# A linear-attention and shrink kernel: another way to compute the shrink, and seven products for eight in three more units

## The chip, the cores and the metric

The kernel runs on one core of one Trainium2 chip. Its time is the device time of one execution in microseconds (us). Four runs of the kernel before gave a median of 559.51 us, from 558.82 to 560.05. A core has TensorE (matrix products, PE in the profile, its weight loads PEld), VectorE (DVE), ScalarE (ACT), GpSimd (POOL), and SyncE (SP), whose queue issues most DMAs here.

## The reference

A recurrent linear attention with gates (GLA), followed by two dense layers with the shrink x - tanh(x) between them. All in 4-byte floats in the kernel; the dense weights come as 8-byte floats.

```
# q, k, v, alpha: (4, 8, 768, 48)
for t in range(S):
    state = alpha[:, :, t, :, None] * state + einsum('bhd,bhe->bhde', k[:, :, t], v[:, :, t])
    y[:, :, t] = einsum('bhd,bhde->bhe', q[:, :, t], state)
x = y.transpose(0, 2, 1, 3).reshape(3072, 384)
h = x @ w_in                # (384, 2048)
g = h - tanh(h)
return g @ w_out            # (2048, 384)
```

## The kernel before

The 3072 rows are worked in 12 units of 256 rows (`NU`, `TU`); a unit is two chunks of 128 rows. For each unit there is a GLA part and a dense part (`moe`). The GLA part of a unit runs some one and a half units ahead of its dense part.

The GLA part loads q, k and alpha so that VectorE can transpose them in blocks (`widen` on ScalarE, then `flip`), makes running products of alpha by two scans (`scan_U`, `scan_W`), multiplies k and q by them, and then needs TensorE for the scores, the new state and the result, which is `xT` of the unit (`scores`, `masked`, `mid`, `state`, `x`, `rest`).

The dense part of a unit has 8 steps (`FS`), each for 256 of the 2048 columns of `w_in`:

- the first product `h` = w_in.T x, 256 columns of w_in by 256 rows, over three tiles of 128 features (`KT`). In units 0 to 5 it is six products of 256 columns (`first`, L1256). From unit 6 on (`SEVEN = 6`) the first two feature tiles are taken as a 2 by 2 product of 128-blocks with seven products of 128 columns instead of eight, the third tile as two products of 256 columns (`seven_a`, `product`, `seven_d`, `seven_e`, L1267 and L1288). The seven products need sums of weight blocks (`weigh`) and of row blocks (`mix`). One PSUM bank holds `h`; four partial sums are copied out of it by ScalarE in three copies between the products (`keep`, L1278 and L1280), and VectorE adds them to the bank's content at the end (`join`, L1293);
- the shrink: u is a multiple of h squared (`square`, ScalarE, L1299), z a square of a linear function of u (`quadratic`, ScalarE, L1303), w = h u (`cube`, VectorE, L1308), g = (z + constant) w (`shrunk`, VectorE, L1312). So g is a polynomial of h that stands for h - tanh(h) while h is small. After every second step ScalarE checks that all u were small enough (`large`, L1318); if one was not, the whole result is computed again by a general path;
- the second product g times w_out. In units 0 and 1 (`PLAIN = 2`) four products of 384 columns (L1336); from unit 2 on seven products of 192 columns (L1358), of sums of blocks of g (`sums`, L1325 and L1326) and of weights (`combine`).

At the end of a unit, `store` adds up the output banks (L1418 on ScalarE, four times L1421 on VectorE) and writes out four pieces by DMA.

The weights come in 16 pieces through four buffers; ScalarE and VectorE turn the 8-byte floats into 4-byte floats (`round_weight`, L88, L89 on ScalarE, L91, L92 on VectorE). Later all pieces are loaded once more and ScalarE looks whether a value was out of range (`too_wide`, L106, L107).

Every piece of work is a task with a name, an engine, and what it comes after. The order in which the tasks are issued is written out by hand: `Planner.STEPS` holds it as differences of task numbers. So each engine's queue, in which instructions run strictly in order, is fixed by that list. PSUM has two banks with the tag "h", in turn for `h` of the steps and for results of the GLA part. The tiles `u`, `w` and `z` have two buffers, `g` three.

Of the kernel before, what the change touches and what calls it, by code (L numbers as in the profile page):

```python
# [1 line left out]

# [14 lines left out]
P = 128  # L17
# [12 lines left out]
U_FAST = 1.0 / 32  # L30
QA, QB, QK = 0.2301250865552381, -0.2896718893320786, 0.24942350940007277
# [39 lines left out]
def round_weight(nc, pool, raw, dst):  # L71

    V, A = nc.vector, nc.scalar
    n = dst.shape[-1]
    if raw.dtype == FP32:  # L80
        A.mul(dst, raw.rearrange("p (j n) -> p j n", n=n), W_SCALE)
        yield
        return
    lo, hi = words(raw)
    bits = pool.tile([P, WN], I32, name="bits")
    more = pool.tile([P, WN], I32, name="more")
    halves = more.bitcast(mybir.dt.int16).rearrange("p (n two) -> p n two", two=2)
    A.activation(halves[:, :, 0], lo, AF.Copy, scale=2.0 ** -29)  # L88
    A.activation(halves[:, :, 1].bitcast(mybir.dt.float16), hi.bitcast(FP32), AF.Sign)  # L89
    yield  # L90
    V.tensor_scalar(out=bits, in0=hi, scalar1=3, scalar2=None, op0=ALU.logical_shift_left)  # L91
    V.tensor_add(dst.bitcast(I32), bits.rearrange("p (j n) -> p j n", n=n),  # L92
                 more.rearrange("p (j n) -> p j n", n=n))
# [6 lines left out]
def too_wide(nc, junk, raw, most, least):  # L100


    A = nc.scalar
    junk = junk[:, 0:WN]
    src = raw if raw.dtype == FP32 else words(raw)[1].bitcast(FP32)
    A.activation(junk, src, AF.Abs, accum_out=most)  # L106
    A.activation(junk, junk, AF.Relu, scale=-1.0, bias=LEAST if raw.dtype != FP32 else -1.0, accum_out=least)  # L107
# [214 lines left out]
class Planner:  # L322
# [6 lines left out]
        "90 2 -1 3 -1 3 4 -3 9 26 -37 8 30 -26 7 -10 -6 12 24 -29 12 1 -17 -101 99 20 -10 -1 4 8 3 5 -26 9 2 23 -7 -5 -121 127 12 -3 -18 24 -7 -137 114 7 13 14 "  # L329
        "-24 6 -129 114 -110 120 -122 142 2 -1 367 -387 10 -132 145 365 -506 131 381 -5 -375 2 375 -511 137 373 -366 -139 143 364 3 -514 144 -137 509 -371 370 "  # L330
        "-513 515 3 -372 -2 -141 144 -146 7 140 5 363 -512 520 -5 -508 -5 514 -10 -501 -2 7 507 -370 -141 515 -376 382 -2 -512 137 -4 -138 143 371 -374 365 5 "
        "-507 -2 7 136 376 -516 511 10 -514 511 -516 515 -5 7 -12 -502 -2 7 512 6 -522 135 383 -511 -5 134 381 -9 11 -509 513 -520 2 519 -387 391 -520 -2 519 "
        "-11 -505 520 -518 127 392 -4 -5 -382 392 -519 508 -507 520 -1 4 -394 -2 4 -1 399 -401 396 -523 524 -366 -27 404 -6 -368 -29 -131 532 -20 -354 -26 403 "
        "-374 368 -10 -360 365 -391 397 -367 377 -15 -391 402 1 -392 -6 -2 389 -361 366 -396 406 2 2 -404 25 381 -407 2 -4 55 340 9 6 -386 -19 -7 402 -347 353 "
        "6 3 -4 -350 -53 405 -404 -3 8 408 -396 390 2 -361 360 -363 347 -372 391 3 2 -1 -412 23 384 -389 3 26 349 -377 -21 5 -2 401 -378 -25 23 392 -563 174 "
        "391 -390 344 -350 -168 175 390 -564 566 2 -3 -9 -365 -15 -1 -24 416 -415 25 16 -40 409 -380 16 -18 43 -26 7 365 -391 21 26 -44 2 12 376 -344 -43 386 "
        "-346 -45 23 376 -6 -571 230 343 -1 -367 373 -577 584 -3 -2 -1 -572 199 368 7 11 -364 347 -376 387 2 -12 17 2 -8 10 -3 -5 11 -396 5 374 7 -582 588 11 "
        "-405 399 -3 -589 594 -1 -18 24 -408 -198 610 -3 1 -607 204 397 -600 587 -366 -41 43 388 -4 -601 246 -24 390 -611 605 -431 25 28 367 8 5 -432 74 339 18 "
        "-388 394 4 -21 13 6 -389 21 367 -10 6 -608 221 -25 418 5 -400 -218 249 366 10 -380 374 -397 -24 23 400 -13 18 -423 21 2 394 8 -12 14 -3 -5 -371 378 -6 "
        "10 -632 630 -14 -615 199 433 2 -1 2 3 -440 -1 3 2 434 -433 443 -417 410 2 -1 3 -642 224 428 -6 -645 224 422 1 -27 32 4 -28 12 2 12 -1 -428 423 1 10 "  # L340
        "-658 241 -14 -25 23 3 15 -42 -200 633 25 -456 458 -428 427 -412 394 12 -382 -18 411 -420 -243 654 -383 376 13 -410 414 -663 273 387 11 -7 3 -419 -4 "
        "421 -390 379 12 -395 401 -426 422 6 -1 -12 -414 -246 668 6 -425 2 -250 674 -448 49 393 8 -452 5 -2 -2 459 -7 2 -1 3 -1 -679 690 -9 3 -683 685 -436 435 "
        "6 -17 13 -436 441 1 -5 7 3 -4 2 9 -6 2 -1 -698 680 24 -703 705 -1 6 -3 -8 1 -451 462 2 -1 5 -451 2 -17 -25 -225 251 21 25 388 32 4 -720 255 437 -467 "
        "52 427 -456 -22 492 -1 -417 406 -453 459 -444 431 -448 3 43 -22 432 -706 718 -6 8 3 -722 254 14 32 -45 457 -442 26 427 -451 -22 21 454 -5 4 -448 -2 "
        "-273 728 -3 -5 -419 -300 735 -10 3 2 -451 450 3 -1 -456 458 3 -10 12 -1 -461 463 1 -463 -276 741 -740 253 -1 24 17 6 449 -494 487 -463 -308 773 -1 3 "
        "-450 460 -6 2 -7 -418 -325 749 -450 432 -408 432 2 -756 758 19 -16 -457 451 -5 -420 414 24 -17 11 -436 -49 486 -481 17 465 14 -483 442 32 10 -6 -804 "
        "354 -322 779 -480 445 36 -24 25 -477 447 13 5 13 -12 -12 -431 438 30 -12 -12 25 -12 -482 495 -38 26 13 -25 13 -485 487 26 -15 -12 -21 49 -515 500 -11 "
        "1 26 -15 16 -15 16 -44 29 16 -15 2 -1 3 12 -45 46 -542 543 -15 16 -32 18 16 7 -555 1 514 32 9 -551 569 -571 554 -41 59 -26 -32 41 -552 570 -26 9 -531 "
        "549 -17 -528 546 -17 -532 533 17 -46 30 17 -16 28 -11 -15 -1 28 -59 34 -1 -32 47 12 -58 33 26 -12 -553 555 -1 2 10 -9 -36 -504 -40 24 521 45 -589 590 "
        "-547 548 -590 544 1 46 -30 -537 16 552 10 18 -24 -34 -492 493 40 -10 -29 57 -27 -569 579 -559 577 -43 -510 536 18 -17 -26 27 17 -16 32 -15 -574 558 "  # L350
        "-14 31 -551 535 17 -30 14 -583 21 24 555 -15 -1 -31 48 12 -614 -1 4 552 32 17 -33 32 3 26 -44 -16 43 -611 569 -571 631 -59 31 11 18 -615 570 28 -600 "
        "618 -17 -28 29 17 -16 17 -617 24 577 17 1 -17 -597 566 16 -15 31 17 -614 599 -602 628 -10 28 -17 -44 16 19 -1 11 17 -61 45 -28 -599 644 -16 -11 -34 1 "
        "61 -45 29 -11 28 -16 -45 46 16 -624 625 -16 17 -30 -618 632 -639 656 -15 -1 17 -15 17 8 -643 2 581 -623 624 60 -7 24 -16 -26 -34 -553 630 -76 60 -12 "
        "-649 678 -16 -686 641 62 -28 12 -686 703 -658 596 63 -17 1 -12 29 -654 638 17 -632 -32 600 76 -75 47 -32 61 -12 -15 -621 588 97 -48 28 -16 -8 -52 -611 "
        "612 60 -44 33 -19 31 15 -28 -31 45 -30 45 -14 15 -28 -635 603 15 -14 60 -27 12 16 -695 696 -718 702 17 -714 -7 705 30 -13 -15 -34 63 -30 -32 49 -701 "
        "731 -26 10 -62 1 78 -62 46 -14 1 -675 689 -713 -1 730 -62 47 16 -15 16 -15 16 -50 -678 729 -731 732 -17 -687 638 1 31 -17 -704 739 17 -15 -1 17 -34 "
        "-18 56 -758 703 -705 -3 709 51 -50 51 -760 768 -25 43 -25 8 -44 62 -43 -18 37 7 18 -61 44 -766 723 61 -758 741 18 -61 -702 746 18 -17 -746 764 -17 18 "
        "-17 -31 49 -17 -748 750 -1 17 -15 19 -3 9 -758 2 748 -51 60 -59 -741 742 59 -26 42 -15 -44 34 26 -15 -44 -733 768 10 15 -14 -778 793 -819 759 -712 773 "
        "-819 804 16 1 -62 46 -753 770 -779 791 -28 -32 34 -33 48 12 -59 -726 786 -12 28 -15 -60 51 -21 31 -13 -32 60 19 -78 45 -13 28 -14 -31 46 -60 32 29 -60 "
        "14 47 -16 -12 29 -16 17 -814 798 -32 34 28 -61 48 14 -61 31 31 -14 30 -869 792 62 16 -30 -32 33 -816 818 12 -31 47 -62 33 30 -62 15 31 -45 62 -29 13 "  # L360
        "17 -848 832 17 1 -17 -33 -795 846 -50 -819 852 -831 -23 872 -16 -1 21 -3 9 -25 17 -52 -819 820 -825 860 -19 44 -8 25 -896 880 -7 -37 61 -16 -44 -842 2 "
# [72 lines left out]
def fast(tc, q, k, v, alpha, moe_w_in, moe_w_out, out, w_in, w_out, ident, ok, pad_rows):  # L434
# [7 lines left out]
    NU = B * UPB  # L442
    KT, d_ff = w_in.shape[1], w_in.shape[2]
    FT, d_model = w_out.shape[1], w_out.shape[2]
    FS = FT // 2
    NH = d_model // 2
    PLAIN = 2
    SEVEN = 6
    BOTH_QUEUES = 0
    V, A, T, GP = nc.vector, nc.scalar, nc.tensor, nc.gpsimd  # L450

    out_r = out.rearrange("(t p) n -> t p n", p=P)

    with ExitStack() as ctx:
# [782 lines left out]
        def moe(u, rank, gait):  # L1237
# [6 lines left out]
            def step(s):  # L1244
# [37 lines left out]
                def seven_d():  # L1282
                    for n, to in ((2, 0), (3, 1), (4, 2)):
                        product(n, to)
# [269 lines left out]
```

## Time and profile before

The profiled execution took 561.18 us, of which 559.4 us are the span from the first instruction to the last.

| what | value |
|---|---|
| median of four runs | 559.51 us |
| profiled execution, its span | 561.18 us, 559.4 us |
| granted TensorE clock | 0.999 |
| VectorE: `cube` (L1308) | 96 x 0.68 us |
| VectorE: `shrunk` (L1312) | 96 x 0.683 us |
| ScalarE: `square` (L1299), `quadratic` (L1303) | 96 x 0.609 us, 96 x 0.630 us |
| ScalarE: `large` (L1318) | 48 x 1.054 us |
| VectorE: `flip` (L699) | 120 x 0.625 us |

In the page, an engine's busy time is the time in which at least one of its instructions runs. Two instructions of one engine overlap a little, so the sum of an engine's durations is more than its busy time. A matmul of 4-byte floats is two instructions, each with a weight load. In the rows of groups, the first number after the bar is the group's busy time, then the mean of one in ns, and after the second bar how long the engine was idle just before, with what ended it.

### The profile page before, as it was taken

The page shows a single profiled execution, that of the slowest core. Times are in us where ns is not written, and L with a number is a line of the kernel's source. Part 1 is how long each engine was busy: PE and PEld are TensorE (multiplying, and loading weights), DVE is VectorE, ACT ScalarE, POOL GpSimd, SP SyncE. Part 2 cuts the span into 40 slices and gives each one's busy share as a digit, 9 for nine tenths or more (in the row PEclk, how much of TensorE's full clock was granted, in tenths as well). Part 3 has the DMA queues.
Part 4 walks back from the last instruction along what each step waited for, and adds up shares of the span by engine and source line. Part 5 has one row for each costly group of instructions (what it writes and reads, how often), then busy time and mean ns, then how long its engine had stood idle before and what let it go on. Part 6 is the DMA issues. An engine that isn't in the chain of part 4 may idle for free. (4 is left out here: it accounts for less than half of the span.)

```text
span 559.4 us, 14664 instructions
## 1 busy us (share of the span) xinstructions
PE 547.2 (98%) x6045; PEld 496.0 (89%) x6045; DVE 462.5 (83%) x853; ACT 357.7 (64%) x722; POOL 4.9 (1%) x23
## 2 busy tenths in 40 slices
PE   8999999999999999999999999999999999999995
PEld 6786677778998999999999999999999999999995
DVE  7978889999998498588896799999899856765764
ACT  3688996648676766776794556767555544545550
POOL 3000000000000000000000000000000000000000
PEclk9999999999999999999999999999999999999999
DMA  9899882135582483453550041221100100000001
GB/s 237 189 248 247 271 176 58 30 93 142 107 166 65 106 196 116 114 127 121 163 144 0 30 94 30 61 62 30 47 19 1 31 8 3 29 8 1 29 2 33
DMA packets 60233, 50.86 MB, mean 91 GB/s; under 512 B 35552, under 2 KB 49920, under 8 KB 60160
## 3 DMA queue, kind: packets, MB, share of 16 engines
q1 hardware_dynamic: 57536, 49.07, 35.0%
q8 instruction: 49, 0.80, 0.6%
q10 hardware_dynamic: 2624, 0.79, 0.6%
q14 instruction: 24, 0.20, 0.1%
HBM read 44.04 MB, written 4.72 MB: 87 GB/s over the span
## 5 line engine op out<-in xcount | busy, mean ns | idle before, releaser
L1256 PE MATMUL h<-xT,w_in 128*128 128x256 f32 (+1 forms) x588 | 131.4, 378 | 2.8 <-DVE w_in L92 2.0
L1256 PEld LDWEIGHTS h<-xT,w_in 128*128 128x128 f32 x588 | 108.3, 190 | 18.9 <-DVE w_in L92 3.6
L1358 PE MATMUL o<-b,e 128*128 128x192 f32 x480 | 93.2, 326 | 0.0
L1358 PEld LDWEIGHTS o<-b,e 128*128 128x128 f32 x480 | 78.9, 190 | 0.4
L1358 PE MATMUL o<-w_out,e 128*128 128x192 f32 x320 | 78.6, 328 | 0.1
L1312 DVE SCALAR_TENSOR_TENSOR g<-z,w 128x512 f32<-128x512 f32 x96 | 64.8, 683 | 6.0 <-ACT z L1303 2.3
L1358 PE MATMUL o<-b,g 128*128 128x192 f32 x320 | 68.7, 326 | 0.0
L1303 ACT ACTIVATE z<-u 128x512 f32<-128x512 f32 x96 | 60.3, 630 | 4.2 <-DVE g L1312 2.6
L1293 DVE TENSOR_TENSOR w<-h,u 128x512 f32<-128x512 f32 x48 | 33.0, 688 | 34.1 <-PE h L1288 34.1
L1299 ACT ACTIVATE u<-w 128x512 f32<-128x512 f32 x48 | 30.0, 627 | 41.9 <-DVE w L1293 41.7
L1358 PEld LDWEIGHTS o<-w_out,e 128*128 128x128 f32 x320 | 55.0, 190 | 1.5 <-issue 0.2
L1267 PE MATMUL h<-xT,w_in 128*128 128x128 f32 x288 | 54.7, 277 | 0.2
L1280 ACT COPY u<-h 128x128 f32<-128x128 f32 x96 | 24.6, 266 | 46.8 <-PE h L1267 46.6
L1358 PEld LDWEIGHTS o<-b,g 128*128 128x128 f32 x320 | 53.8, 190 | 0.1
L1267 PE MATMUL h<-xT,w_out 128*128 128x128 f32 x288 | 53.3, 275 | 0.0
L1318 ACT ACTIVATE big<-u 128x1024 f32<-128x1024 f32 x48 | 50.6, 1054 | 0.6
L1267 PEld LDWEIGHTS h<-xT,w_in 128*128 128x128 f32 x288 | 48.1, 190 | 2.4 <-ACT xT L1038 0.4
L1288 PE MATMUL h<-xT,w_in 128*128 128x256 f32 x192 | 48.9, 380 | 0.0
L1299 ACT ACTIVATE u<-h 128x512 f32<-128x512 f32 x48 | 28.3, 590 | 29.8 <-PE h L1256 29.6
L1325 DVE TENSOR_TENSOR e<-g 128x384 f32<-128x384 f32 x80 | 44.0, 550 | 2.6 <-PE o L1358 0.8
L1308 DVE TENSOR_TENSOR w<-h,u 128x512 f32<-128x512 f32 x48 | 32.5, 681 | 14.8 <-ACT u L1299 14.8
L1267 PEld LDWEIGHTS h<-xT,w_out 128*128 128x128 f32 x288 | 44.1, 192 | 0.1
(171 smaller groups left out, 967.7 us busy)
## 6 DMA issues: line engine op xcount, KB each, us to landing
raw<-in_moe_w_out_dram SPq DMA_DIRECT2D x16, 768.0 KB, 5.9
raw<-in_moe_w_in_dram SPq DMA_DIRECT2D x48, 96.0 KB, 5.2
raw<-in_moe_w_in_dram SPq DMA_DIRECT2D x16, 288.0 KB, 5.2
vt<-in_v_dram SPq DMA_DIRECT2D x23, 192.0 KB, 3.6
ar<-in_alpha_dram SPq DMA_DIRECT2D x20, 192.0 KB, 3.4
kr<-in_k_dram SPq DMA_DIRECT2D x20, 192.0 KB, 3.3
qr<-in_q_dram SPq DMA_DIRECT2D x20, 192.0 KB, 3.2
raw<-in_moe_w_in_dram SPq DMA_DIRECT2D x16, 192.0 KB, 6.0
```

What stands on the lines that cost most here:

```text
L1256: T.matmul(h[:, a, to], lhsT=w_in[:, j, f * P:(f + 1) * P], rhs=xT[u][:, j, to], start=(j == 0), stop=(j == KT - 1))
L1267: T.matmul(m["h", s][:, to], lhsT=left[n][:, s], rhs=right[u][n], start=start, stop=True, skip_group_check=True)
L1280: A.copy(m["kept", s][:, n], m["h", s][:, 3])
L1288: T.matmul(m["h", s][:, 2 * a:2 * a + 2].rearrange("p i t -> p (i t)"), lhsT=wi[:, KT - 1, s, a], rhs=xT[u][:, KT - 1, :], start=False, st ...
L1293: V.tensor_add(m["w", s], m["h", s].rearrange("p i t -> p (i t)"), m["u", s])
L1299: A.activation(m["u", s], m["h", s], AF.Square, scale=W_SCALE ** -1.5)
L1303: A.activation(m["z", s], m["u", s], AF.Square, bias=QB, scale=QA * W_SCALE)
L1308: V.tensor_mul(m["w", s], m["h", s], m["u", s])
L1312: V.scalar_tensor_tensor(out=g.rearrange("p a c t -> p (a c t)"), in0=m["z", s], scalar=QK, in1=m["w", s], op0=ALU.add, op1=ALU.mult)
L1318: A.activation(big, m["us", s // 2].rearrange("p s t -> p (s t)"), AF.Relu, bias=-U_FAST, scale=W_SCALE, accum_out=over[:, n:n + 1])
L1325: V.tensor_sub(e[:, 0:3, :], x[:, 3:4].to_broadcast([P, 3, P]), x[:, 0:3])
L1358: T.matmul(o[n][:, i], lhsT=g_, rhs=w_, start=(s_ == 0 and (n, i) in ((0, 0), (1, 0), (2, 1), (3, 0))), stop=(s_ == FS - 1), skip_group_ch ...
```

## The change

Five things are changed:

1. The shrink. ScalarE computes z = tanh(TA h), then z = arctan(TB z), then u, a multiple of z squared (`bend`, `turn`, `square`); VectorE multiplies once, g = h u (`shrunk`). `cube` and `quadratic` are gone. The check `large` compares with the new function's value at the same h.
2. `SEVEN` is 3: units 3, 4 and 5 too take seven products.
3. The seven products use two banks. Four go into the four quarters of a first bank (`seven_a`); ScalarE copies one quarter out, and VectorE makes the four partial sums with three additions (`partial`). The other three and the third feature tile go into a second bank (`seven_b`); `join` adds the two.
4. Tasks are cut finer: the two ScalarE reads and the two VectorE operations of a weight piece, the two copies of `widen`, the four transposes of `flip`, the halves of the scans of units 1 to 11, the two looks at a reloaded piece, the five operations of a unit's `store`. In the last unit the last operation is done in two halves, each with its own DMAs right behind it. The looks write over the piece that they read instead of using another tile.
5. `STEPS` is another list, for the new tasks.

```diff
-U_FAST = 1.0 / 32
-QA, QB, QK = 0.2301250865552381, -0.2896718893320786, 0.24942350940007277
+TA, TB, TK = 0.524562418460846, 1.0865100622177124, 1.0129976272583008
+F_FAST = (TK * atan(TB * tanh(TA * 2.0 ** -2.5))) ** 2
...
-    SEVEN = 6
+    SEVEN = 3
...
                 def seven_a():
-                    m["h", s] = ps_h.tile([P, 4, P], FP32, name="h")
-                    product(1, 3, True)
-                    product(5, 1)
-
-                def keep(n):
-                    if n == 0:
-                        take_u()
-                        m["kept", s] = m["u", s].rearrange("p (i t) -> p i t", t=P)
-                        A.copy(m["kept", s][:, 0::3], m["h", s][:, 3::-2])
-                    else:
-                        A.copy(m["kept", s][:, n], m["h", s][:, 3])
-
-                def seven_d():
-                    for n, to in ((2, 0), (3, 1), (4, 2)):
-                        product(n, to)
-
-                def seven_e():
+                    h = m["part", s] = ps_h.tile([P, 4, P], FP32, name="h")
+                    for i, n in enumerate((1, 6, 7, 5)):
+                        T.matmul(h[:, i], lhsT=left[n][:, s], rhs=right[u][n], start=i == 0, stop=True, skip_group_check=True)
+
+                def keep():
+                    take_u()
+                    m["kept", s] = m["u", s].rearrange("p (i t) -> p i t", t=P)
+                    A.copy(m["kept", s][:, 0], m["part", s][:, 0])
+
+                def partial():
+                    kept, part = m["kept", s], m["part", s]
+                    V.tensor_add(kept[:, 1], kept[:, 0], part[:, 1])
+                    V.tensor_add(kept[:, 2], kept[:, 1], part[:, 2])
+                    V.tensor_add(kept[:, 1::2], kept[:, 1:3], part[:, 3:4].to_broadcast([P, 2, P]))
+
+                def seven_b():
+                    h = m["h", s] = ps_h.tile([P, 4, P], FP32, name="h")
+                    for i, n in enumerate((2, 3, 4)):
+                        T.matmul(h[:, i], lhsT=left[n][:, s], rhs=right[u][n], start=i == 0, stop=True, skip_group_check=True)
                     for a in range(2):
-                        T.matmul(m["h", s][:, 2 * a:2 * a + 2].rearrange("p i t -> p (i t)"), lhsT=wi[:, KT - 1, s, a], rhs=xT[u][:, KT - 1, :],
+                        T.matmul(h[:, 2 * a:2 * a + 2].rearrange("p i t -> p (i t)"), lhsT=wi[:, KT - 1, s, a], rhs=xT[u][:, KT - 1, :],
                                  start=False, stop=True, skip_group_check=True)
...
+                def bend():
+                    m["z", s] = two.tile([P, 2 * TU], FP32, name="z")
+                    A.activation(m["z", s], m["h", s], AF.Tanh, scale=TA / W_SCALE)
+
+                def turn():
+                    A.activation(m["z", s], m["z", s], AF.Arctan, scale=TB)
+
                 def square():
                     if not seven:
                         take_u()
-                    A.activation(m["u", s], m["h", s], AF.Square, scale=W_SCALE ** -1.5)
-
-                def quadratic():
-                    m["z", s] = two.tile([P, 2 * TU], FP32, name="z")
-                    A.activation(m["z", s], m["u", s], AF.Square, bias=QB, scale=QA * W_SCALE)
-
-                def cube():
-                    if not seven:
-                        m["w", s] = two.tile([P, 2 * TU], FP32, name="w")
-                    V.tensor_mul(m["w", s], m["h", s], m["u", s])
+                    A.activation(m["u", s], m["z", s], AF.Square, scale=TK * W_SCALE ** -0.5)
 
                 def shrunk():
                     g = m["g", s] = three.tile([P, 2, CU, P], FP32, name="g")
-                    V.scalar_tensor_tensor(out=g.rearrange("p a c t -> p (a c t)"), in0=m["z", s], scalar=QK,
-                                           in1=m["w", s], op0=ALU.add, op1=ALU.mult)
+                    V.tensor_mul(g.rearrange("p a c t -> p (a c t)"), m["h", s], m["u", s])
...
-            add(f"read {what}{s}", "ACT", 2.1, rank, [f"fetch {what}{s}", both and f"upper {what}{s}", older and f"{older[0]}{older[1]}"], a)
-            add(f"{what}{s}", "DVE", 1.6, rank, [f"read {what}{s}"], b)
+            add(f"read_a {what}{s}", "ACT", 1.05, rank, there, lambda do=do: do(0))
+            add(f"read {what}{s}", "ACT", 1.05, rank, [f"read_a {what}{s}"], lambda do=do: do(1))
+            add(f"bits {what}{s}", "DVE", 0.6, rank, there, lambda do=do: do(2))
+            add(f"{what}{s}", "DVE", 1.0, rank, [f"read {what}{s}", f"bits {what}{s}"], lambda do=do: do(3))
...
+                elif u < NU - 1:
+                    put(same, o[0][:, 0:1, :].to_broadcast([P, 2, NH]), ALU.add, same, 0)
+                else:
                     for c in range(CU):
...
+                        put(same[:, c], o[0][:, 0, :], ALU.add, same[:, c], 0, [c])
```

## The prediction

> **What bounds the kernel now.** I read the page's first part, then busy time by stretches of 20 us, then the timeline of single engines where it is densest. The first line is the whole span; the others give a stretch's length and, in it, busy us of TensorE (PE), its weight loads (PEld), VectorE (DVE), ScalarE (ACT), POOL, then the granted clock and the DMA share.
>
> ```profile
> PE 547.2 (98%) x6045; PEld 496.0 (89%) x6045; DVE 462.5 (83%) x853; ACT 357.7 (64%) x722; POOL 4.9 (1%) x23
> ```
>
> ```profile
> 60.00:80.00 20.00, 19.32 (x76) 14.16 (x75) 16.53 (x28) 19.73 (x30) 0.00 (x0) 1.00 0.86 219
> ...
> 120.00:140.00 20.00, 20.00 (x199) 16.59 (x198) 19.95 (x32) 14.19 (x26) 0.00 (x0) 1.00 0.47 124
> 140.00:160.00 20.00, 20.00 (x224) 18.52 (x223) 20.00 (x35) 14.29 (x28) 0.00 (x0) 1.00 0.62 124
> ...
> 360.00:380.00 20.00, 19.91 (x137) 19.36 (x136) 19.68 (x40) 13.84 (x34) 0.00 (x0) 1.00 0.27 66
> ```
>
> TensorE is hardly ever out of work after the first 60 us; no other engine sets the end. A busy TensorE need not be one at its best, so I looked at where its matmuls start (start, length, engine, line, what, instructions). A 4-byte product is two instructions.
>
> ```profile
> 132.02 5.36 PE L1256 MATMUL h<-xT,w_in 128*128 128x256 f32 x24
> 137.22 0.49 PE L1358 MATMUL o<-w_out,e 128*128 128x192 f32 x2
> ```
>
> ```profile
> 407.42 0.38 PE L1267 MATMUL h<-xT,w_out 128*128 128x128 f32 x2
> 407.64 0.39 PE L1267 MATMUL h<-xT,w_in 128*128 128x128 f32 x2
> 407.87 0.39 PE L1267 MATMUL h<-xT,w_out 128*128 128x128 f32 x2
> 408.09 0.39 PE L1267 MATMUL h<-more_x,w_in 128*128 128x128 f32 x2
> 408.31 0.49 PE L1358 MATMUL o<-b,e 128*128 128x192 f32 x2
> ```
>
> Twelve products of 256 columns take 137.22 - 132.02 = 5.20 us, 0.433 each. Four of 128 columns take 408.31 - 407.42 = 0.89 us, 0.223 each. Nothing is lost between them: the stream is paid by the column. The time is therefore TensorE's columns plus what it waits, and the wait is small: the late starts in its timeline add up to some 7 us, 4.5 of them before 60 us.
>
> **The change, part by part.**
>
> TensorE, units 3 to 5 (24 steps). A step's first product now has six products of 256 columns, 6 x 0.433 = 2.60 us. In seven products it has 7 x 0.223 + 2 x 0.433 = 2.43 us. That is 0.17 less, and 24 x 0.17 = **-4.1 us**. In the lists of instructions all other TensorE work is the same in number and shape, units 6 to 11 too: there the seven products only change banks and order. These microseconds are on the path.
>
> The Trainium skill speaks against this term ("TensorE: Matmul & The Clock Gate", The mechanism): a weight load overlaps running matmuls only when it goes to other rows of the array, and these all use 128 rows. The new step has 18 loads for 12. With the page's P/1.2, 107 ns for 128 columns, six open loads in 24 steps would add 15.4 us, an estimate, and turn the term into +11. The four products above decide against it: eight loads lie inside 0.89 us.
>
> VectorE. Rows (mean ns of one before the second bar):
>
> ```profile
> L1293 DVE TENSOR_TENSOR w<-h,u 128x512 f32<-128x512 f32 x48 | 33.0, 688 | 34.1 <-PE h L1288 34.1
> L1308 DVE TENSOR_TENSOR w<-w,u 128x512 f32<-128x512 f32 x48 | 32.5, 683 | 2.4 <-ACT u L1299 2.4
> L1326 DVE TENSOR_TENSOR e<-g 128x256 f32<-128x256 f32 x80 | 33.3, 416 | 0.0
> ```
>
> ```profile
> 415.86 0.30 DVE L1217 TENSOR_TENSOR xT<-xT 128x128 f32<-128x128 f32 x1
> 416.19 0.29 DVE L1218 TENSOR_TENSOR xT<-xT 128x128 f32<-128x128 f32 x1
> 416.51 0.29 DVE L1219 TENSOR_TENSOR more_x<-xT 128x128 f32<-128x128 f32 x1
> 416.72 0.28 DVE L1220 TENSOR_TENSOR xT<-xT 128x128 f32<-128x128 f32 x1
> ```
>
> An instruction that uses the result of the one ahead starts 0.32 to 0.33 us after it (the first three); one that doesn't starts 0.08 before the other's end (the last). Gone: 96 cubes at 0.68 - 0.08, -57.6. Added: a join in 24 more steps at 0.61, +14.6; the three additions of `partial` in 72 steps, two dependent ones of 128 and one of 256 columns, 0.33 + 0.33 + 0.34 = 1.00, +72 (0.21 + 0.21 + 0.34 = 0.76 if nothing waits, +55; I take 1.00, since each reads what the last wrote); `mix` in three more units at 1.05, +3. Halving the scans costs a start each, +1. Net +33 us (+16 at the low end): 462.5 becomes some 495 of 556, 89%. It is all beside TensorE, but not evenly. Adding VectorE's rows in the new order, from the second product of unit 3 to that of unit 10, gives 286 us where TensorE's rows give 297: 96% full (84% in the order of before). The cover is thin there; its loss is the first rival.
>
> ScalarE. Square, square becomes tanh, arctan, square: one instruction of 512 more in 96 steps. The trace has neither function. From below, the check of 1024 columns takes 1.05, 0.53 for 512; from above, the sign of 768 columns takes 1.06, 0.71 for 512. I take the row of the same shape:
>
> ```profile
> L1303 ACT ACTIVATE z<-u 128x512 f32<-128x512 f32 x96 | 60.3, 630 | 4.2 <-DVE g L1312 2.6
> L1280 ACT COPY u<-h 128x128 f32<-128x128 f32 x96 | 24.6, 266 | 46.8 <-PE h L1267 46.6
> ```
>
> That adds 96 x 0.63 = 60.5. The three copies of a seven step (0.37 + 2 x 0.27, 48 steps, 43.3) become one of 0.27 in 72 steps (19.2). Net +36 (at the ends 26 and 52, with both new functions): 394 of 556 us, 71%. Beside TensorE; without that cover it is +0.63 a step.
>
> The functions need a loaded table. The trace has one load, 1.28 us, and the new program's list has one as well, ahead of its first activation. The Trainium skill ("ScalarE: Activation LUTs", Table sets) puts tanh and arctan in one set, and no run here shows it yet.
>
> A step's chain after its first product grows: join 0.69, three activations 0.63 to 0.66, product 0.68, sums 0.89, so 4.2 us where it was 3.6 (join, square, cube, shrunk, sums). In the new order TensorE has at least 7.8 us of other work between a seven step's first and second product, mostly 12 to 25, so this costs nothing. The partial products' bank comes free after a copy (0.27) and `partial` (1.00): 1.3 us and two handovers, covered by the second products of an older step, 7 x 0.326 = 2.3 us. Behind a waiting `partial` stand VectorE's joins and sums, which have the 7.8 us. In return TensorE no longer waits for three copies within a step; it hardly waited (0.3 us at most at one place), so no gain.
>
> Splits of reads, copies, transposes and scans move starts by under 1 us on engines with room. A weight's fetch now also waits for `bits` on VectorE, which comes beside the ScalarE read: 0. The last store goes out in halves of 192 columns: the last DMA starts some 0.2 us sooner, -0.2. The store's four DMAs stay four on SP's queue. The looks write over what they read, so they no longer share a buffer with the checks: 0. The new order can take away at most the 7 us of TensorE waits or add some; with a VectorE this full I put +0.5.
>
> Sum: -4.1 - 0.2 + 0.5 = -3.8. The profiled execution took 561.18 us, with a span of 559.4 and 1.8 around it; it lies 1.7 above the median of the runs, 559.51. I take the difference off the median: **555.7**.
>
> **Rivals.**
>
> VectorE becomes the bound between units 3 and 10. For it: 286 us of work for 297, and in the stretch from 320 to 440 us of before its rows, laid end to end, fill 93%. If 93% is all that a queue in order with two partners can be filled, 286 / 0.93 = 308 us, 11 more than TensorE needs: 559.5 - 4.3 + 11 = 566. It decides from 96% on: with `partial` at 0.76 the load is 92% and the rival is dead. Against it: from 80 to 160 us the same sum gives 97%, and TensorE was busy all 20.00 of 20.00. Chance 0.14.
>
> ScalarE is late in the first 80 us. It was busy 17.6 and 19.7 of 20 us from 40 to 80, and the 16 steps of units 0 and 1 (28 to 118 us) gain 10 us of work. If all of that falls before 80, 7 us don't fit and TensorE waits for them: 559.5 - 4.3 + 7 = 562. It decides from 2.7 us of extra work in that stretch, some four steps. Against it: from 80 to 140 ScalarE idles 20 us, so the checks and copies for later units can move there. Chance 0.07.
>
> New waits eat the gain, 3 to 5 us of them in several places: 559.5. Chance 0.10.
>
> The new order also removes most of the early waits: 559.5 - 4.3 - 4 = 551. Chance 0.09.
>
> That the change doesn't do what it says, two tables instead of one: 192 loads of 1.28 us, 246 us of ScalarE, near 700 us. One load in the list makes this all but excluded.
>
> **How the numbers follow.** The forecast has 0.60, with 553.5 to 558.2 as its own range: 4.1 us less or more by the third digit of the two spacings (0.5), waits of 0 to 2. A measurement here tells about 0.2% (1.1 us) from no change. Faster is the forecast, the better order and a third of the eaten gain: 0.72. Within 0.2% is half of the eaten gain and a little of the rivals: 0.08. Slower is the rest, 0.20. Leaving out under half of the first rival above and half of the better order below gives 552.5 to 562.
>
> **What would show it.** The seven products of units 3 to 5 at 0.22 a product; TensorE over 98% busy in every stretch from 80 us on; VectorE near 490, ScalarE near 394 us; the second and third additions of `partial` 0.33 us after the one ahead; one table load. I am wrong if TensorE idles after 120 us for VectorE, if products of 128 columns spread beyond 0.23, or if an activation takes over 0.7 us.

## The result, and the profile after

The kernel after took 560.31 us (median of 44 runs, 557.68 to 564.68), the kernel before on the same chips 559.43 (67 runs). The ratio is 1.0019, with a 95% interval of 1.0010 to 1.0028: slower by a hair. 555.7 was forecast.

The profiled execution of after took 559.43 us, with a span of 557.7. The first line of its page, and ScalarE's rows of the new work (mean ns of one before the second bar):

```profile
PE 543.8 (98%) x6191; PEld 497.7 (89%) x6191; DVE 484.9 (87%) x1032; ACT 392.6 (70%) x746; POOL 4.9 (1%) x23
```

```profile
L1326 ACT ACTIVATE z<-w 128x512 f32<-128x512 f32 x72 | 45.1, 626 | 54.4 <-DVE w L1321 54.4
...
L1329 ACT ACTIVATE z<-z 128x512 f32<-128x512 f32 x96 | 60.4, 630 | 1.9
L1334 ACT ACTIVATE u<-z 128x512 f32<-128x512 f32 x96 | 60.3, 628 | 1.9
```

Tanh, arctan and square cost the same in these rows. ScalarE has become as busy as forecast, VectorE nearly so (484.9 us, 495 were forecast), and TensorE has less to do. Yet in busy time by stretches TensorE is no longer always busy (columns as before: length, then busy us of PE, PEld, DVE, ACT, POOL, granted clock, DMA share):

```profile
60.00:80.00 20.00, 20.00 (x79) 14.80 (x78) 11.33 (x18) 18.23 (x28) 0.00 (x0) 1.00 0.82 219
120.00:140.00 20.00, 20.00 (x109) 16.39 (x101) 19.74 (x33) 15.53 (x28) 0.00 (x0) 1.00 0.45 119
...
200.00:220.00 20.00, 19.03 (x224) 17.88 (x223) 18.00 (x44) 17.14 (x36) 0.00 (x0) 1.00 0.40 110
...
260.00:280.00 20.00, 18.16 (x239) 17.08 (x239) 18.26 (x39) 14.38 (x30) 0.00 (x0) 1.00 0.29 82
360.00:380.00 20.00, 20.00 (x158) 19.62 (x150) 19.27 (x48) 11.89 (x24) 0.00 (x0) 1.00 0.21 50
```

The two stretches with 1 and 1.8 us missing lie in units 3 to 5, which took the seven products. A second trace of the kernel before has TensorE busy all the time there:

```profile
200.00:220.00 20.00, 20.00 (x210) 18.68 (x209) 17.72 (x34) 14.35 (x28) 0.00 (x0) 1.00 0.58 159
260.00:280.00 20.00, 20.00 (x223) 18.11 (x222) 17.13 (x32) 15.40 (x31) 0.00 (x0) 1.00 0.47 140
```

To close the account I took each matmul's distance to the next start. What goes beyond the usual distance of its kind is a late start (dense instructions: 0.112, 0.163, 0.216, 0.323 us for 128, 192, 256, 384 columns; the small ones of attention: the median over equal shapes). For before I use its second trace, whose time, 559.16 us, is close to the median; the first was 1.7 above it. The table counts every late start, those of attention's small products too, so its sum for before, 27 us, is larger than the 7 us of waits that the prediction names.

| us | before | after | difference |
|---|---|---|---|
| dense products at their usual distance | 464.99 | 461.15 | -3.84 |
| attention's products at theirs | 57.47 | 57.36 | -0.11 |
| late starts, 0 to 23 us | 6.71 | 6.66 | -0.05 |
| 23 to 60 | 5.02 | 6.25 | +1.23 |
| 60 to 180 | 4.30 | 3.52 | -0.78 |
| **180 to 300** | **3.04** | **8.30** | **+5.26** |
| 300 to 360 | 3.81 | 2.41 | -1.40 |
| 360 to the end | 4.23 | 4.33 | +0.10 |
| ahead of the first and behind the last product | 7.84 | 7.70 | -0.14 |
| span | 557.4 | 557.7 | +0.3 |

So the columns brought what they should, 3.84 us, and TensorE lost 4.4 us in late starts (the six rows of late starts together): 5.3 more from 180 to 300 us, the time of the units in question, and 0.9 less elsewhere. The largest one, on TensorE and then on VectorE (start, length, engine, line, what, idle time before and what ended it):

```profile
258.60 1.03 PE L1316 MATMUL h<-xT,w_in 128*128 128x256 f32 x4
261.39 0.49 PE L1314 MATMUL h<-xT,w_in 128*128 128x128 f32 x2 [1.75 <-DVE w L1321]
```

```profile
258.64 0.68 DVE L1338 TENSOR_TENSOR g<-w,u 128x512 f32<-128x512 f32 x1
259.25 0.16 DVE L804 TENSOR_TENSOR ends<-U,low 128x8 f32<-128x8 f32 x1
259.44 0.20 DVE L805 RECIPROCAL before<-ends 128x8 f32<-128x8 f32 x1
259.56 0.24 DVE L1046 COPY xT<-sc 112x128 f32<-112x128 f32 x1
259.72 0.68 DVE L911 TENSOR_TENSOR pm<-sc,within 128x512 f32<-128x512 f32 x1
260.31 0.34 DVE L1095 TENSOR_TENSOR mid<-state,sc 112x192 f32<-112x192 f32 x1
260.58 0.16 DVE L808 TENSOR_REDUCE least<-U 128x1 f32<-128x8 f32 x1
260.65 0.68 DVE L1321 TENSOR_TENSOR w<-h,u 128x512 f32<-128x512 f32 x1
```

The second half of a step (`first 5:2`) needs the bank that `join 5:1` (L1321) empties. Its products were done at 259.6, but VectorE runs without a gap through six pieces of attention before it gets to that join. TensorE stands still, although behind the waiting products second products of unit 4 are ready. At 204 us the new `mix` waits for a DMA, and the first product of unit 4 for `mix`:

```profile
204.07 0.38 PE L1298 MATMUL h<-xT,w_in 128*128 128x128 f32 x2
205.33 0.49 PE L1298 MATMUL h<-xT,w_out 128*128 128x128 f32 x2 [0.87 <-DVE xT L1245]
```

```profile
204.65 0.29 DVE L1244 TENSOR_TENSOR xT<-xT 128x128 f32<-128x128 f32 x1 [1.62 <-DMA xT<-xT]
204.98 0.29 DVE L1245 TENSOR_TENSOR xT<-xT 128x128 f32<-128x128 f32 x1
```

### The profile page after: what moved, and what is told of

Same layout as the page of the kernel before. It is cut to its first block, busy times and chain, and to the rows that moved or that the text cites. A ratio compares the mean times of both kernels' runs of the same rounds, so it can differ in the third digit from the quotient of the medians.

```text
span 557.7 us, 15127 instructions
## 1 busy us (share of the span) xinstructions
PE 543.8 (98%) x6191; PEld 497.7 (89%) x6191; DVE 484.9 (87%) x1032; ACT 392.6 (70%) x746; POOL 4.9 (1%) x23
## 5 line engine op out<-in xcount | busy, mean ns | idle before, releaser
L1326 ACT ACTIVATE z<-w 128x512 f32<-128x512 f32 x72 | 45.1, 626 | 54.4 <-DVE w L1321 54.4
L1316 PE MATMUL h<-xT,w_in 128*128 128x256 f32 x288 | 74.1, 380 | 0.0
L1285 PE MATMUL h<-xT,w_in 128*128 128x256 f32 (+1 forms) x300 | 66.2, 374 | 2.0 <-DVE g L1338 1.7
L1285 PEld LDWEIGHTS h<-xT,w_in 128*128 128x128 f32 x300 | 54.4, 190 | 10.9 <-DVE g L1338 1.8
L1329 ACT ACTIVATE z<-z 128x512 f32<-128x512 f32 x96 | 60.4, 630 | 1.9
L1334 ACT ACTIVATE u<-z 128x512 f32<-128x512 f32 x96 | 60.3, 628 | 1.9
L1321 DVE TENSOR_TENSOR w<-h,u 128x512 f32<-128x512 f32 x72 | 49.1, 681 | 11.4 <-PE h L1316 10.8
L1298 PE MATMUL h<-xT,w_out 128*128 128x128 f32 x288 | 55.8, 275 | 0.9 <-DVE xT L1245 0.9
L1338 DVE TENSOR_TENSOR g<-w,u 128x512 f32<-128x512 f32 x72 | 48.9, 681 | 4.4 <-ACT u L1334 4.0
L1316 PEld LDWEIGHTS h<-xT,w_in 128*128 128x128 f32 x288 | 49.2, 191 | 3.7
L1298 PEld LDWEIGHTS h<-xT,w_in 128*128 128x128 f32 x288 | 46.6, 191 | 2.4 <-DVE w L1321 0.8
L1303 ACT COPY u<-h 128x128 f32<-128x128 f32 x72 | 18.7, 262 | 37.9 <-PE h L1298 32.8
```

What stands on the lines that cost most here:

```text
L1285: T.matmul(h[:, a, to], lhsT=w_in[:, j, f * P:(f + 1) * P], rhs=xT[u][:, j, to], start=(j == 0), stop=(j == KT - 1))
L1298: T.matmul(h[:, i], lhsT=left[n][:, s], rhs=right[u][n], start=i == 0, stop=True, skip_group_check=True)
L1303: A.copy(m["kept", s][:, 0], m["part", s][:, 0])
L1316: T.matmul(h[:, 2 * a:2 * a + 2].rearrange("p i t -> p (i t)"), lhsT=wi[:, KT - 1, s, a], rhs=xT[u][:, KT - 1, :], start=False, stop=True, ...
L1321: V.tensor_add(m["w", s], m["h", s].rearrange("p i t -> p (i t)"), m["u", s])
L1326: A.activation(m["z", s], m["h", s], AF.Tanh, scale=TA / W_SCALE)
```

## The experiments

The main theory (V in the first four expectations): between units 3 and 10 VectorE is full and hands banks and sums over late, and this ate the gain. Times are medians; every ratio is to the kernel before, run on the same chip beside it. The variants ran on several chips, and the interval of a ratio is some 0.2% either way, so a difference between the medians of two variants is good to about 1 us.

### The changed kernel again

No edit.

> The changed kernel once more, beside the others on one chip. Theory V (VectorE is too full between units 3 and 7 and TensorE waits for it): TensorE idles 3 to 5 us between 200 and 320 us of the span, as in the first profile (1.0, 1.9, 0.6 us at single places), and hardly elsewhere after 60 us. Rival S (the loss sits in the first 60 us): it varies there and not between 200 and 320. Rival C (a lower granted clock): the waits are the same as before, and the clock of the runs is 0.1 to 0.3% under that of the kernel before. Time 560.3 us, ratio 1.001 to 1.003.

559.66 us (12 runs), ratio 1.0009 [0.9996, 1.0023]. The trace has the same late starts at the same places: 0.87 us at 204, 1.89 at 259, 0.62 at 263 (1.03, 1.92 and 0.62 in the first trace; the idle time in the rows above is some 0.15 less). They belong to the program, not to one execution.

### Units 3 to 5 with six products again

```diff
+    REAL = 6
@@ seven_a, keep, partial, mix
+                    if u < REAL:
+                        return
@@ seven_b
+                    if u < REAL:
+                        first()
+                        return
@@ join
+                    if u < REAL:
+                        V.tensor_copy(m["w", s], m["h", s])
```

Units 3 to 5 multiply by weight blocks that were already changed for the seven products, so their rows of the output are not the reference's.

> The new order and the new shrink, but units 3 to 5 take six products of 256 columns again, with no partial sums and no mix there; the join of those units becomes a plain copy, so that the bank comes free as early. TensorE gets 4.1 us more, VectorE some 27 us less (24 x 1.0 of partial, 3 x 1.05 of mix). V: the waits for VectorE between 200 and 320 us fall under 1 us, and the time stays within 1 us of the changed kernel's, 559.5 to 561. S or C: nothing is won back, 560.3 + 4.1 = 564.4 us.

562.17 us, ratio 1.0064 [1.0040, 1.0088]. The dense products are back at 464.99 us, late starts of dense products between 180 and 300 us fall from 5.35 to 2.78. So the seven products of these units are worth 2.5 us net (562.17 - 559.66) of 3.84 by the medians, 1.4 by the spans of the two traces. In the second trace of before these late starts are 0.83: of the 4.5 us that came in this stretch 2.6 go with the seven products, and 2 stay with the other parts of the change. Those parts of the change, with the new order, cost 3.0 us by these medians; the trace of this run shows the wait of 1.7 us near 30 us that after has too. The result lies between the two expectations.

### Filling the gaps between dependent additions

`partial`'s three additions depend on each other. Here the next VectorE task in the list, if what it comes after has been issued, is issued behind the first and the second addition.

```diff
-                    do()
+                    for n in range(3):
+                        do(n)
+                        j = follower(at) if n < 2 else None
+                        if j is not None:
+                            queue[j][2]()
```

> The same arithmetic and tasks; where the next VectorE task may run already, its instructions are issued between the three dependent additions of a partial sum, so that an addition no longer waits 0.12 us for the one ahead. VectorE gains up to 72 x 2 x 0.12 = 17 us, some 8 to 12 where a task is there to put between. V: most of the waits between 200 and 320 us go, 556 to 558.5 us. S or C: no change, 560.3 us.

565.54 us, ratio 1.0126 [1.0095, 1.0157]: a miss. VectorE's busy time fell by 6 us, but tasks that had come later in the queue now came before their data. VectorE's waits from 180 to 440 us (waiting for; us in total, times, longest), here, then in the repeat of after:

```profile
DVE w L1323 <- PE h L1318: 6.1, 11, 1.1
DVE u L1308 <- ACT u L1303: 4.3, 6, 0.9
```

```profile
DVE w L1321 <- PE h L1316: 1.5, 3, 0.8
...
DVE u L1307 <- ACT u L1303: 0.8, 2, 0.5
```

A join that is pulled forward waits for TensorE, and holds up the additions behind it, which were to empty a bank. In a queue that runs in order, an instruction that comes too early can cost time as a long one does.

### More work for VectorE

```diff
+                    if u < 10:
+                        V.tensor_max(mask, mask, mask)
```

behind each `partial` of units 3 to 9: 56 unused instructions of 0.21 us, 11.8 us.

> One more VectorE instruction of 128 columns behind each partial sum of units 3 to 9, which nothing uses: 56 x 0.21 = 11.8 us of VectorE and nothing else. V: VectorE is full there, so 5 to 11 us of it come out at the end, 565 to 571 us. S or C: VectorE has room, within 1 us of the changed kernel.

566.76 us, ratio 1.0126 [1.0105, 1.0147], as the theory has it: of 11.8 us more work 7.1 come out in the time. The wait at 259 us grew to 3.05.

### Less work for VectorE

```diff
-                    V.tensor_add(kept[:, 1], kept[:, 0], part[:, 1])
-                    V.tensor_add(kept[:, 2], kept[:, 1], part[:, 2])
-                    V.tensor_add(kept[:, 1::2], kept[:, 1:3], part[:, 3:4].to_broadcast([P, 2, P]))
+                    V.tensor_add(kept[:, 1:], part[:, 1:], kept[:, 0:1].to_broadcast([P, 3, P]))
```

> The changed kernel with the three additions after the first four products put into one of 128x384 (0.55 us, by the row of that width, for 1.00): the middle sums are left out, so units 3 to 11 don't give the reference's output, while every product, bank, copy and place in the order stays. VectorE 485 - 72 x 0.4 = about 455 us. Theory 'VectorE is full between units 3 and 10' (11.8 us more work cost 7 us): what it hands over late comes in time; late starts of dense products fall from 9 to 6.5 us or less, time 555 to 557.5, near the 555.7 of the prediction. Rival 'two banks a step make TensorE wait however short the additions are': late starts stay at 8 to 9.5 us, time 558.8 to 560.3.

557.92 us, ratio 0.9964 [0.9947, 0.9981]; VectorE busy 459.6 us. It falls between the two: late starts of dense products are 7.2 us (9.0 to 9.4 in after), the wait at 259 us is 0.95. So VectorE's length is worth some 1.7 us by the medians (2.5 by the two ratios), not all of what was lost.

### The second subtraction of the sums on GpSimd

```diff
-                    V.tensor_sub(e[:, 3:5, :], x[:, 0:1].to_broadcast([P, 2, P]), x[:, 1:3])
+                    GP.tensor_sub(e[:, 3:5, :], x[:, 0:1].to_broadcast([P, 2, P]), x[:, 1:3])
```

> The changed kernel with the second subtraction of each step's sums (128x256, 0.42 us on VectorE, 72 of them) on GpSimd: 30 us of work leave VectorE, which is left with 455 us. No trace shows this subtraction on GpSimd. Theory 'VectorE is full': 555 to 557.5 if GpSimd takes up to 2 us for one (the sums have over 8 us until the second products read them). Rival 'the two engines hinder each other': VectorE's other instructions take longer while GpSimd works, VectorE stays as busy as before or more, 560 us or more.

557.73 us, ratio 0.9970 [0.9953, 0.9987]. The expectation counted 72; there are 80, in units 2 to 11. On GpSimd one takes 1.03 us, 0.42 on VectorE:

```profile
L1351 POOL TENSOR_TENSOR e<-g 128x256 f32<-128x256 f32 x80 | 82.0, 1026 | 458.2 <-DVE g L1338 379.2
```

The gain is that of the lighter additions.

### Second products moved ahead on TensorE

Only the list of the order is changed: in TensorE's queue three parts of the second product 3:4 go ahead of the first product of unit 4, three of 4:6 and 4:7 ahead of `first 5:2`.

```diff
-first_a 4:0, first 4:0, second_1 3:4, second_2 3:4, second 3:4
+second_1 3:4, second_2 3:4, second 3:4, first_a 4:0, first 4:0
...
-first 5:2, second_2 4:6, first_a 5:3, second 4:6, second_0 4:7
+second_2 4:6, second 4:6, second_0 4:7, first 5:2, first_a 5:3
```

> The changed kernel with six parts of second products moved ahead of a waiting first product in TensorE's order: three of step 3:4 ahead of the first product of unit 4 (which waits near 204 us for the mixed columns), three of steps 4:6 and 4:7 ahead of the second half of step 5:2 (which waits 1.9 us near 259 us for a bank that a late addition on VectorE frees). Nothing else moves. Theory 'local waits' (TensorE has other work at hand where it waits, and VectorE has room to catch up within a few us): waits of 0.9 + 0.2, 1.9 and 0.6 us go, late starts fall from 9.4 to 6 to 6.5 us, time 556.5 to 558. Rival 'VectorE is full from 220 to 440 us': what TensorE gains it waits again within the next 20 to 40 us; late starts stay at 8 to 9.5 us, time 559 to 560.5.

557.65 us, ratio 0.9976 [0.9960, 0.9992]. This is the time that the theory of local waits expected: 2 us come back with the same VectorE work. The late starts of dense products fall to 7.3 us, not to the 6 to 6.5 expected. TensorE's busy time in the two stretches:

```profile
200.00:220.00 20.00, 19.52 (x227) 18.11 (x226) 18.49 (x42) 17.28 (x36) 0.00 (x0) 1.00 0.56 130
260.00:280.00 20.00, 19.22 (x245) 17.74 (x244) 19.00 (x44) 15.62 (x35) 0.00 (x0) 1.00 0.25 76
```

19.03 became 19.52, and 18.16 became 19.22. The rest did what the rival said: new waits of 0.64 us at 216 and 0.81 at 268, for additions of `partial`.

### Two more sets of moves

First, with the six: `join 5:1` ahead of two pieces of attention, and the first `shrunk` of the kernel ahead of a scan.

> The same, and two moves on VectorE: the addition of step 5:1 that frees that bank ahead of two pieces of attention, and the first shrunk rows of the kernel ahead of a scan (TensorE waits 1.9 us for them near 30 us). Theory 'local waits': another 0.5 to 1.2 us less than with the moves on TensorE alone, 555.5 to 557.5, late starts 5 to 6 us. Rival 'VectorE is full': as the changed kernel, 559 to 560.5; in the first 60 us weights that arrive set the pace, and nothing is gained there either.

557.77 us, ratio 0.9971 [0.9951, 0.9992], no better than the six. The wait near 30 us fell from 1.9 to 0.8, but 0.5 of it came back at 38. Second, with the six: `second_0 3:6` ahead of `first_a 4:2`, `second_1 4:7` ahead of `first_a 5:4`.

> The kernel with six second products moved ahead in TensorE's order, and two more: one of step 3:6 ahead of the first product of 4:2 (which waited 0.6 us near 216 us), one of step 4:7 ahead of that of 5:4 (0.8 us near 268 us). Theory 'local waits': 0.5 to 1.2 us less than with six moved, 556.4 to 557.2 where those had 557.65. Rival 'VectorE is full': both waits come back a little later, 557.4 to 558.4.

558.7 us, ratio 0.9985 [0.9964, 1.0006]. Nothing gained: late starts of dense products 7.5 us, against 7.3 with the six. Beyond the six, moving work only moved the waits.

### Both repairs

The six moves, `shrunk` ahead of the scan, and the subtraction on GpSimd.

> The changed kernel with the six second products moved ahead, the first shrunk rows ahead of a scan, and the second subtraction of the sums on GpSimd: the version that should beat both kernels. If the two repairs take different waits away, they add: 559.7 - 2.0 - 1.9 = about 555.8 us. If both relieve the same late handovers of VectorE between 200 and 300 us, little is added: 556.8 to 558 us. Late starts of dense products 6 to 7 us either way; the waits of 1 us and more near 30, 204 and 259 us gone.

556.38 us, ratio 0.9953 [0.9935, 0.9972]: 2.6 us faster than before, 3.3 faster than after. By the medians the repairs nearly add up (2.0 + 1.9); times good to 1 us don't show that alone. The traces agree with it: the late starts of dense products, 9.0 to 9.4 us in after, are 7.3 with the six moves, 8.4 with GpSimd and 6.4 with both, as many as in the second trace of before. This version beats both kernels.

### The kernel before again, and the new shrink alone

> The kernel before, unchanged, as a measure of what two sets of runs of one program differ by, and for a second trace of it. All theories: ratio 0.998 to 1.002, VectorE 425 us, ScalarE near 357 us. If the one trace at hand is typical, late starts of the dense products come to 6 to 8 us again and the small products of attention to 78 to 79 us. Theory 'clock' (the changed kernel is granted a lower TensorE clock): the runs of this kernel list 0.997 to 0.999 and none below 0.994, where 9 of 58 runs of the changed kernel listed 0.988 to 0.993.

559.0 us, ratio 0.9999 [0.9989, 1.0008]; late starts of dense products 6.4 us. The second kernel has the old order and the old seven products with the new shrink; in 14 steps VectorE also copies h out of its bank:

```diff
-                    A.activation(m["u", s], m["h", s], AF.Square, scale=W_SCALE ** -1.5)
+                    A.activation(m["u", s], m["h", s], AF.Tanh, scale=TA / W_SCALE)
...
-                    A.activation(m["z", s], m["u", s], AF.Square, bias=QB, scale=QA * W_SCALE)
+                    A.activation(m["u", s], m["u", s], AF.Arctan, scale=TB)
+                    A.activation(m["u", s], m["u", s], AF.Square, scale=TK * W_SCALE ** -0.5)
...
-                    V.scalar_tensor_tensor(out=g.rearrange("p a c t -> p (a c t)"), in0=m["z", s], scalar=QK,
-                                           in1=m["w", s], op0=ALU.add, op1=ALU.mult)
+                    V.tensor_mul(g.rearrange("p a c t -> p (a c t)"), m["h", s], m["u", s])
```

> The order, and the units with seven products, as before; only the shrink is the new one (ScalarE: tanh, arctan and square on one tile; VectorE: one product). In 14 steps, whose bank is claimed again early in the old order, VectorE copies the hidden rows out first, 14 x 0.6 = 8 us. All theories: dense products 465 us in the accounting of starts, VectorE 425 - 58 + 8 = about 375 us, ScalarE near 393 us. Theory 'waits for VectorE by the bank' (what ate the gain is units 3 to 5, where VectorE has to empty two banks a step): this kernel has no such step more, so it stays at 558.5 to 560.5 us. Rival 'the longer chain on ScalarE costs the time': it shows here alone, 561.5 to 564 us, with waits of TensorE for the shrunk rows.

581.93 us, ratio 1.0404 [1.0389, 1.0419]: both theories missed it by far. VectorE was at 417 us and ScalarE at 418. VectorE's 375 was forecast from 425 us, but both traces of before have 462.4 to 462.5, which gives 413. ScalarE's figure was forecast from after, where two of three copies of a seven step are gone; here all three are left. TensorE's weight loads waited (waiting for; us, times, longest):

```profile
PEld h L1273 <- ACT u L1286: 6.8, 9, 1.2
...
PEld h L1273 <- ACT u L1284: 4.5, 7, 1.0
```

L1284 and L1286 are the copies out of the single bank, between a step's products; they stand in ScalarE's queue behind longer shrinks. TensorE itself idled 6.6 us for these copies, of some 23 us lost; the rest is spread over waits for weights, for attention's copies and for shrunk rows, and was not taken apart. That the new shrink needs the second bank or another order is likely, but not shown. What it would cost alone in an order of its own was not tried.

### The clock in the first 25 us

Of 141 executions in the new order (after and its variants so far) 21 list a mean clock of 0.988 to 0.993, and none of the 130 listed in the old one (0.996 at least). To see whether an idle TensorE near 12 us brings it down, the unused products in front of that gap were taken out of after, and five were added, in after and in the version with both repairs:

```diff
             if name == "update 0.0":
+                while filled and filled[-1][3] is None:
+                    filled.pop()
```

```diff
             if name == "update 0.0":
+                filled += [(free, -1, do, None)] * 5
```

> The changed kernel without the three unused products that stand ahead of that update: the gap grows from 1.0 to 1.9 us to 1.9 to 2.8. Theory 'the gap brings the clock down': six or more in 12 runs below 0.995, and the median 2 to 4 us above the changed kernel, 561.5 to 564. Rival: one or two in 12, 559.6 to 560.3.

562.33 us, ratio 1.0037 [1.0018, 1.0056]; 9 of 12 runs at 0.988 to 0.993. Its trace by stretches (the column before the last two is the granted clock):

```profile
12.00:15.00 3.00, 1.21 (x23) 1.16 (x23) 2.27 (x3) 0.78 (x2) 0.00 (x0) 1.00 1.12 274
15.00:18.00 3.00, 3.00 (x28) 2.52 (x24) 2.03 (x4) 2.95 (x7) 0.00 (x0) 0.64 0.66 148
18.00:21.00 3.00, 3.00 (x27) 2.01 (x25) 2.23 (x4) 0.43 (x1) 0.00 (x0) 0.50 1.00 212
```

TensorE idles 2.1 us from 11.7 to 13.8, and from about 15.8 to 22.6 us the clock is halved. The three runs with a higher clock took 557.94 to 559.90 us, as after does. So a longer gap brings the lower clock far more often. The traces of the new order say the same: the clock is halved in all four with gaps of 1.80 to 2.54 us there, and in none of the nine with 0.54 to 1.52; the one with 1.88 (the repeat of after) kept the full clock. What decides in a single execution is not shown.

> The changed kernel with five more unused 128x128 products ahead of the update of the first state, where TensorE stands idle 1.0 to 1.9 us near 11.5 to 13.4 us of the span. Theory 'the gap brings the clock down': no run below 0.995 (without the products 20 of 139 were), median down by 0.2 to 0.4 against the changed kernel, 559.2 to 559.8, no run above 562. Rival 'chance, or something outside the kernel': one or two in 12 below 0.995, median as the changed kernel's, 559.6 to 560.3.

> The version with both repairs (556.38 us, one of 10 runs below 0.995) and the five more products. Theory 'the gap brings the clock down': none below 0.995, median 556.0 to 556.4. Rival: one or two below, 556.4 or more.

561.41 us, ratio 1.0045 [1.0021, 1.0068], one of 7 runs at 0.992; and 558.66 us, ratio 0.9995 [0.9982, 1.0007], none of 12. The clock stays up in 18 of 19, but too few for proof, and the times got worse, against the expectation: the gap of 1 us now lies between the added products, and dense products start 0.25 to 1 us late near 52 us. Why the medians rose by 1 to 2.3 us was not followed further.

For the question at hand the share is small. Without its eight runs below 0.994, after's median is 560.13 instead of 560.31: 0.2 us of the 0.9.

## Why the prediction was wrong, point by point

**TensorE, -4.1 us.** Right in mechanism and nearly in size: -3.84. In unit 5, products of 128 columns start 0.23 and 0.22 us apart, and two of 256 take 0.86:

```profile
261.71 0.39 PE L1314 MATMUL h<-xT,w_out 128*128 128x128 f32 x2
261.94 0.39 PE L1314 MATMUL h<-more_x,w_in 128*128 128x128 f32 x2
262.16 1.03 PE L1316 MATMUL h<-xT,w_in 128*128 128x256 f32 x4
263.02 0.33 PE L1383 MATMUL o<-b,e 128*128 128x192 f32 x1
```

The rule that the prediction took from the page "TensorE: Matmul & The Clock Gate" of the Trainium skill (The mechanism), overlap only across row groups, would have had open weight loads here. The rows above show none: each of these products has two loads, and starts 0.22 to 0.23 us after the one ahead. (The same section also names a background weight buffer as a way to overlap, which the prediction left out.)

**VectorE, 495 us and 96% full.** 484.9. `partial` takes 0.96 us in the trace (from 252.58 to the next start at 253.54) where 1.00 was taken:

```profile
252.58 0.26 DVE L1307 TENSOR_TENSOR u<-u,h 128x128 f32<-128x128 f32 x1
252.88 0.29 DVE L1308 TENSOR_TENSOR u<-u,h 128x128 f32<-128x128 f32 x1
253.20 0.42 DVE L1309 TENSOR_TENSOR u<-u,h 128x256 f32<-128x256 f32 x1
253.54 0.64 DVE L717 STREAM_TRANSPOSE qT<-qr 128x256 f32<-128x256 f32 x1
```

The 1.00 was counted from start to start. Busy time leaves out the idle time ahead of the dependent additions, 2.5 us in each of two rows, half of the 10 us that VectorE came out lower:

```profile
L1308 DVE TENSOR_TENSOR u<-u,h 128x128 f32<-128x128 f32 x72 | 20.7, 287 | 2.5
L1309 DVE TENSOR_TENSOR u<-u,h 128x256 f32<-128x256 f32 x72 | 30.3, 421 | 2.5
```

From 180 to 440 us VectorE was busy 250.4 of 260 in the repeat's trace, 96.3%.

**ScalarE, 394 us, 0.63 an activation, one table load.** 392.6; 0.626 and 0.630; one load of 1.28 us. That tanh and arctan lie in one set ("ScalarE: Activation LUTs", Table sets, of the Trainium skill) agrees with it.

**The last store, -0.2.** -0.1, for the stretches ahead of the first product and behind the last one together.

**New waits, +0.5, and "It is all beside TensorE".** This is the step that failed: late starts grew by 4.4 us where 0.5 was put. TensorE idled after 120 us for VectorE, which the prediction named as a sign of being wrong. It failed in two sentences. "Behind a waiting `partial` stand VectorE's joins and sums, which have the 7.8 us": a join feeds the second product, which has 7.8 us and more, but it also empties the step's second bank, and TensorE needs that bank one step later. I measured the slack of the data and not that of the bank. "Covered by the second products of an older step": these were there, but in the order `first 5:2` stands right behind `first 5:1`, and the second products behind it. A cover counts only if it stands between the two in the queue. Moving six pieces of them, three there and three ahead of unit 4's first product, gave back 2.0 us. And `mix` was costed as 1.05 us of VectorE, not as a new link between a DMA and the unit's first product: 0.87 us at 204 us. This names the two largest waits; of the late starts from 180 to 300 us, 2 us stay when units 3 to 5 take six products. The largest of those is 0.79 us near 261 us, again for a join; the others were not taken apart.

**The rivals.** "New waits eat the gain, 3 to 5 us of them in several places: 559.5", with 0.10, is what came. VectorE as the bound (566) did not come, but the kernel stands at its edge: 11.8 us more work cost 7.1, 16 to 25 us less busy time gave 1.7 to 1.9 back. ScalarE late in the first 80 us did not come: from 60 to 80 us TensorE was busy all the time. The +1.2 us of late starts from 23 to 60 are mostly one wait near 30 us for the first shrunk rows, and that is the order of VectorE's queue: ScalarE had ended its square at 29.87, VectorE began the product at 31.67, behind a scan and other work.

```profile
29.24 0.63 ACT L1334 ACTIVATE u<-z 128x512 f32<-128x512 f32 x1
29.75 1.21 DVE L815 TENSOR_TENSOR_SCAN W<-aT,before 128x516 f32<-128x516 f32 x1
31.67 0.68 DVE L1338 TENSOR_TENSOR g<-h,u 128x512 f32<-128x512 f32 x1
32.41 0.92 PE L1285 MATMUL h<-xT,w_in 128*128 128x256 f32 x3 [1.68 <-DVE g L1338]
```

The moves that put this product ahead of a scan left 0.56 us of that idle time.

"The new order removes most of the early waits" came in part elsewhere: -2.2 us from 60 to 180 and from 300 to 360.

**The chances.** With 96% filling named as the point where the first rival decides, 0.10 for eaten gain and 0.60 for the full one were too far apart.

What stays open: what the rest of the change without the seven products costs (3.0 us by medians, 1.6 by the spans of the traces, 559.0 against 557.4), which smaller waits belong to the 2 us that stay from 180 to 300 us without the seven products, and a few tenths between after's median and its trace.

## What to carry to other kernels

For each buffer that passes between two engines, ask when the producer needs it back, not only when the consumer's result is due; a result with 8 us of slack can sit in a bank with none. When an engine without slack shares its queue with other work, hiding work needs a place in the order: look at what stands next behind the instruction that may wait. At 96% filling, 2 of 4 us lost were had back by moving six pieces of second products, without any engine doing less.

## What the runs showed of the hardware

- A gap of about 2 us in TensorE's work early in the kernel was followed, some 2 us later, by half the granted clock for about 7 us, in a part of the executions: in the traces with 1.80, 1.94, 2.08 and 2.54 us, not in one with 1.88 nor in nine with 0.54 to 1.52. It shows in 21 of 141 executions of after and its variants, and in 9 of 12 with three unused products less. Such a run is 2.5 to 4 us longer.
- Work moved to GpSimd freed less of VectorE's time than it had taken there: 80 subtractions of 0.42 us gone, some 0.34 each in the stream, 27 us, but VectorE's busy time fell by 16.4. Of the missing 10.6 us, 7.0 are instructions that took longer: the row that stood ahead of them went from 548 to 595 ns, that of `decay` from 343 to 400.
